# Output and down projection in four column groups, with rows of y as their result

## The chip, the cores and the metric

The kernel runs on one core of a Trainium2 chip. The metric is the device time of one execution in microseconds. Before the change it is 201.81 us, the median of three runs (201.67 to 201.96).

## The reference

A decode step for 8 sequences of one token, D = 512. The input x is layer-normalised, and two branches use the result: sliding-window attention with 32 query heads and 8 key/value heads over the last W = 2048 of 8192 cached positions, and a gated unit with F = 1792. The output joins them.

```python
xn = layernorm(x)                                     # x: [8, 1, 512]
q  = xn @ wq                                          # 32 heads of 128
k, v = the last 2048 rows of the caches, each shared by 4 query heads
o  = softmax(q k^T / sqrt(128)) v
s  = o.reshape(8, 1, 4096) @ wo                       # the output projection, [8, 512]
h  = sigmoid(xn @ w_gate) * (xn @ w_up)               # [8, 1792]
g  = silu(h @ w_down)                                 # the down projection, [8, 512]
return x + s * g
```

All is bfloat16 in memory. The windows of the two caches are 64 MB together and the weights some 14 MB.

## The kernel before, in words

**Loads.** A ring of 14 buffers of 128 x 4096 bf16 (1 MB) takes everything that is read but x: the halves of w_gate, w_up and w_down (896 KB each), four tiles of Wq, 32 tiles of K, 32 of V, and four of Wo. The list is written out by hand: the weights of the unit, Wq, then K tiles with the V tiles seven places behind, then Wo. The transfers are issued in turn from ACT's and from SP's queue (`load`, line 87), each as soon as the tile that had the buffer before is reported as used (`done_with`). The first three Wo tiles are one transfer each; the fourth is cut into two pieces of 512 KB, one for each queue (`wo_parts`, lines 114 to 119). Instructions on an engine are carried out in the order of the program, DMA issues among them. The built program lets all transfers share eight completion semaphores in turn, so that each issue also waits until the transfer eight places before it has landed.

**Start.** x is loaded to eight partitions and normalised; four TensorE transpositions give xnT (line 229), four more give xT, the columns of x (line 238), which DVE copies to SBUF (line 242). The unit (lines 245 to 291): 56 matmuls each for gate and up (line 253) give d_ps, DVE multiplies sigmoid and up to hT (line 270), and 56 matmuls of the down projection (line 278) give b_ps, in which a partition is a column of y: the weights are the stationary operand (128 x 128), hT streams through with 8 columns. Sigmoid and product (lines 288, 290) give gg. Then the q projection (line 297), and the copies of q into a zero-padded buffer qz (line 328), done in turn by ACT and DVE.

**Attention.** Each step n of one loop takes K tile n through DVE's transposition (line 343), the score matmuls of tile n - 1 (line 364: 8 of 512 columns), and the V products of tile n - 7 (line 434: 32 of 8 columns). Every four steps close one sequence: maximum (lines 376 to 389), exponentials on ACT (line 393), transposition of the probabilities (line 407), denominator (lines 415 to 426). A K buffer is free when it has been transposed, a V buffer when its products are done.

**End.** `out_rows` (line 451) brings the attention output from the order of the heads into rows of Wo, with 16 matmuls of an identity in four column groups (32 columns of weights each, placed by `tile_position`), and DVE copies that to o2 (line 461). `out_project` (line 472) runs 128 matmuls, each with a 128 x 128 block of Wo as the stationary operand and 8 columns of o2 streaming; the result a_ps has columns of y on its partitions. Then the product with gg (line 507), the addition of xT (line 509), a TensorE transposition (line 513), a copy (line 517), and one store of 32 rows of 256 bytes from SP's queue (line 518).

Of the kernel before, what the change touches and what calls it, by code (L numbers as in the profile page):

```python
# [10 lines left out]
def kernel(  # L11
# [13 lines left out]
    nc = tc.nc  # L25
    P = 128
    B, _, D = A_x.shape
# [6 lines left out]
    FT = F // P  # L34
    NB = D // P
    HG = Hq // 4
# [18 lines left out]
    bf16 = mybir.dt.bfloat16  # L55
    f32 = mybir.dt.float32
    u32 = mybir.dt.uint32
    AF = mybir.ActivationFunctionType
    ALU = mybir.AluOpType
# [6 lines left out]
    work = ctx.enter_context(tc.tile_pool(name="work", bufs=1))  # L66
# [3 lines left out]
    psum = ctx.enter_context(  # L70
        tc.tile_pool(name="psum", bufs=2, space=bass.MemoryType.PSUM)
    )
# [5 lines left out]
    x_bf = work.tile([B, D], bf16, name="x_bf")  # L78
    nc.sync.dma_start(out=x_bf[:], in_=A_x.flatten_outer_dims())

    queues = [nc.scalar, nc.sync]
# [32 lines left out]
    def wo_parts(h):  # L114
        v = A_wo.rearrange("(hg p j) n -> p hg (j n)", p=P, j=4)
        w = 4 * D
        g0 = h * HG // 4
        cuts = ((0, 2),) if h < 3 else ((0, 1), (1, 2))
        return [(lo * w, hi * w, v[:, g0 + lo : g0 + hi, :]) for lo, hi in cuts]

    loads = []
    for key, w, parts in (
# [9 lines left out]
    for _, kind, m in need:  # L132
        cache = A_v_cache if kind else A_k_cache
        loads.append((("v" if kind else "k", m), lambda cache=cache, m=m: kv_parts(cache, m)))
    loads += [(("wo", h), lambda h=h: wo_parts(h)) for h in range(4)]
    issued = [0]

# [8 lines left out]
    def done_with(*key):  # L146
        used[key] = True
        issue_loads()
# [4 lines left out]
    ident = consts.tile([P, P], bf16, name="ident")  # L153
# [3 lines left out]
    for off in range(-Hq * (NU - 1), Hq * NU, Hq):  # L157
        nc.gpsimd.affine_select(
            out=SumM[:],
            in_=SumM[:],  # L160
# [10 lines left out]
    for j in range(NU):  # L171
# [5 lines left out]
        out=off_rows[:],  # L177
        in_=off_rows[:],
# [9 lines left out]
        out=off_cols[:],  # L188
        in_=off_cols[:],
# [23 lines left out]
        out=rstd[:], in_=mv[:, 1:2], func=AF.Sqrt, bias=eps_t[:], scale=1.0  # L213
# [4 lines left out]
        out=xn_bf[:],  # L218
        in0=x_f[:],
# [8 lines left out]
    for kt in range(KT):  # L228
        nc.tensor.transpose(  # L229
            out=xnT_ps[:, kt, :], in_=xn_bf[:B, kt::KT], identity=ident[:B, :B]  # L230
# [2 lines left out]
    nc.vector.tensor_copy(out=xnT_sb[:], in_=xnT_ps[:])  # L233


    xT_ps = psum.tile([P, NB, B], bf16, name="xT_ps", tag="s1")
    for nb in range(NB):
        nc.tensor.transpose(
            out=xT_ps[:, nb, :], in_=x_bf[:B, nb * P : (nb + 1) * P], identity=ident[:B, :B]
        )  # L240
    xT_sb = work.tile([P, NB, B], f32, name="xT_sb")
    nc.vector.tensor_copy(out=xT_sb[:], in_=xT_ps[:])


    def unit_half(key, tag):
        w_sb = [
            tiles[(key, h)][:, : KT * F // 2].rearrange("p (kt f) -> p kt f", kt=KT // 2)
            for h in range(2)
        ]
        d_ps = psum.tile([P, FT, B], f32, name="d_ps", tag=tag)  # L250
        for t in range(FT):
            for kt in range(KT):
                nc.tensor.matmul(  # L253
                    d_ps[:, t, :],
                    lhsT=w_sb[2 * kt // KT][:, kt % (KT // 2), t::FT],
                    rhs=xnT_sb[:, kt, :],
                    start=(kt == 0),
                    stop=(kt == KT - 1),
                )
        done_with(key, 0)  # L260
        done_with(key, 1)
        return d_ps

    def unit():
        g_ps = unit_half("wg", "s0")
        sig = work.tile([P, FT, B], f32, name="sig")
        nc.scalar.activation(out=sig[:], in_=g_ps[:], func=AF.Sigmoid)
        u_ps = unit_half("wu", "s1")
        hT_sb = work.tile([P, FT, B], bf16, name="hT_sb")
        nc.vector.tensor_tensor(out=hT_sb[:], in0=sig[:], in1=u_ps[:], op=ALU.mult)  # L270
        wd_sb = [
            tiles[("wd", h)][:, : FT * D // 2].rearrange("p (t n) -> p t n", t=FT // 2)
            for h in range(2)
        ]
        b_ps = psum.tile([P, NB, B], f32, name="b_ps", tag="s0")
        for nb in range(NB):
            for t in range(FT):
                nc.tensor.matmul(
                    b_ps[:, nb, :],
                    lhsT=wd_sb[2 * t // FT][:, t % (FT // 2), nb * P : (nb + 1) * P],  # L280
                    rhs=hT_sb[:, t, :],
                    start=(t == 0),
                    stop=(t == FT - 1),
                )
        done_with("wd", 0)
        done_with("wd", 1)
        sigb = work.tile([P, NB, B], f32, name="sigb")
        nc.scalar.activation(out=sigb[:], in_=b_ps[:], func=AF.Sigmoid)
        gg_sb = work.tile([P, NB, B], f32, name="gg_sb")
        nc.vector.tensor_tensor(out=gg_sb[:], in0=sigb[:], in1=b_ps[:], op=ALU.mult)  # L290
        return gg_sb

# [151 lines left out]
        )  # L444


    def out_rows():
        o2_ps = psum1.tile([P, 4, B, HG], f32, name="o2_ps", tag="misc")
        for hl in range(4):
            for j in range(4):  # L450
                nc.tensor.matmul(
                    o2_ps[32 * hl : 32 * (hl + 1), j, :, :],
                    lhsT=ident[:, j::4],
                    rhs=oT_sb[:, :, hl::4],
                    start=True,
                    stop=True,
                    tile_position=(0, 32 * hl),
                    skip_group_check=True,
                )
        o2_sb = work.tile([P, HG, 4, B], bf16, name="o2_sb")  # L460
        nc.vector.tensor_copy(out=o2_sb[:].rearrange("p hg j b -> p j b hg"), in_=o2_ps[:])
        return o2_sb

    def out_project(o2_sb):

        a_ps = psum.tile([P, NB, B], f32, name="a_ps", tag="s0")
        for hg in range(HG):
            w_sb = tiles[("wo", 4 * hg // HG)]
            for j in range(4):
                for nb in range(NB):  # L470
                    c0 = ((hg % (HG // 4)) * 4 + j) * D + nb * P
                    nc.tensor.matmul(  # L472
                        a_ps[:, nb, :],
                        lhsT=w_sb[:, c0 : c0 + P],
                        rhs=o2_sb[:, hg, j, :],
                        start=(hg == 0 and j == 0 and nb == 0),
                        stop=(hg == HG - 1 and j == 3),
                        skip_group_check=True,
                    )
        return a_ps  # L480

    gg_sb = unit()
    q_projection()
    mj_of = {}
    dh_of = {}
    for n in range(NT + V_LAG):
        b, ph = divmod(n - NI, NI)
# [14 lines left out]
            soft_den(b, dh_of.pop(b))  # L502


    a_ps = out_project(out_rows())
    prod = work.tile([P, NB, B], f32, name="prod")
    nc.vector.tensor_tensor(out=prod[:], in0=gg_sb[:], in1=a_ps[:], op=ALU.mult)
    yT_sb = work.tile([P, B, NB], bf16, name="yT_sb")
    nc.vector.tensor_tensor(
        out=yT_sb[:].rearrange("p b nb -> p nb b"), in0=prod[:], in1=xT_sb[:], op=ALU.add  # L510
    )
    y_ps = psum.tile([B * NB, P], bf16, name="y_ps", tag="s1")
    nc.tensor.transpose(
        out=y_ps[:], in_=yT_sb[:].rearrange("p b nb -> p (b nb)"), identity=ident[:, :]
    )
    y_sb = work.tile([B * NB, P], bf16, name="y_sb")
    nc.vector.tensor_copy(out=y_sb[:], in_=y_ps[:])
    nc.sync.dma_start(
        out=out.rearrange("b s (nb n) -> (b s nb) n", n=P), in_=y_sb[:]
    )  # L520


# [28 lines left out]
```

## Time and profile before

| quantity | value |
|---|---|
| time, median of three runs | 201.81 us (201.67 to 201.96) |
| time of the profiled execution | 201.71 us |
| its span, first to last instruction | 200.0 us |
| read from memory | 81.01 MB, 405 GB/s over the span |
| busy: PE, DVE, ACT | 64%, 57%, 9% |
| mean granted TensorE clock | 0.874 |

The span is cut into 40 slices of 5 us in the page's rows by slices: the DMA row is the busy share of the core's 16 DMA engines in tenths, and the GB/s row what they moved. In the chain that ended last each row has a start in us, a length in us, and what took that time; "issue" is time without a cause that the profile shows. In the timeline a row has the start, the length, the engine, the line and operation, the result and operands with their shape (partitions x elements), the number of instructions, and in brackets the idle time before and what ended it. Rows of stretches (us from the span's start) give the busy time of PE, PEld, DVE, ACT and POOL with the number of instructions, then the granted clock, the DMA share and GB/s. PEld is the loading of weights, which overlaps PE. The time from a DMA's issue to its landing is also in the trace, for every transfer.

### The profile page before, as it was taken

To read this page: it belongs to the slowest core of one execution; us is meant where nothing else is said; L and a number is where in the kernel's file an instruction comes from. 1 tells how busy PE (TensorE), PEld (TensorE's weight loads), DVE (VectorE), ACT (ScalarE), POOL (GpSimd) and SP (SyncE) were. 2 spreads that over 40 slices of the span, in tenths; PEclk is the share of its full clock that TensorE was granted. 3 is DMA by queue.
4 is the path that set the end of the run, shared out by engine and by line. 5 is a ranking of instruction groups with operands and counts; after the bars stand their busy time and mean duration, and the time that the engine had idled before them with its cause. 6 is when DMAs were issued, how large, how long until landed. Compare 5 with 4: busy or idle time off the path is not lost.

```text
span 200.0 us, 4098 instructions
## 1 busy us (share of the span) xinstructions
PE 127.2 (64%) x1793; PEld 76.3 (38%) x1793; DVE 114.5 (57%) x199; ACT 18.7 (9%) x46; POOL 14.2 (7%) x25
## 2 busy tenths in 40 slices
PE   0004948004995796996796996369644965594943
PEld 0004946001332443644353553225322633254843
DVE  2001001049998787997977997386746784717221
ACT  0003300040022002002000200110002000202000
POOL 7991000000000000000000000000000000000000
PEclk9999999999999797899888899959995899588555
DMA  6999999999999999999999999999999999999970
GB/s 205 427 425 430 429 421 424 424 428 431 426 423 429 426 426 429 419 426 423 428 421 429 428 424 428 421 429 428 423 428 428 426 419 428 426 421 424 416 299 11
DMA packets 11842, 81.29 MB, mean 406 GB/s; under 512 B 1320, under 2 KB 1328, under 8 KB 3120
## 3 DMA queue, kind: packets, MB, share of 16 engines
q10 hardware_dynamic: 6016, 41.03, 49.1%
q1 hardware_dynamic: 5808, 40.00, 47.5%
q8 instruction: 14, 0.23, 0.4%
q14 instruction: 4, 0.03, 0.0%
HBM read 81.01 MB, written 0.01 MB: 405 GB/s over the span
## 4 chain that ended last, share of the span: by engine, by line
DMA 74%; PE 11%; DVE 9%; ACT 2%; issue 1%; ACTq 1%; DVEq 0%
DMA v_sb<-in_A_v_cache_dram 48%; DMA wo_sb<-in_A_wo_dram 10%; DMA k_sb<-in_A_k_cache_dram 9%; PE s_ps L364 7%; DMA wd_sb<-in_B_w_down_dram 6%; DVE kT_sb L343 5%; PE d_ps L253 2%; DVE qz_sb L328 1%; DVE mxs L376 1%; ACTq L87 1%; ACT qz_sb L328 1%; PE a_ps L472 1%; PE o_ps L434 1%; ACT L212 1%; DVE pT_sb L407 1%
## 5 line engine op out<-in xcount | busy, mean ns | idle before, releaser
L364 PE MATMUL s_ps<-kT_sb,qz_sb 128*128 128x512 bf16 x256 | 74.9, 439 | 12.6 <-DVE kT_sb L343 12.6
L343 DVE STREAM_TRANSPOSE kT_sb<-k_sb 128x1024 uint32<-128x1024 uint32 x64 | 74.6, 1210 | 0.0
L364 PEld LDWEIGHTS <-qz_sb 128*128 128x128 bf16 x256 | 25.4, 110 | 46.8 <-issue 30.9
L434 PEld LDWEIGHTS <-v_sb 128*128 128x128 bf16 x1024 | 30.8, 99 | 6.7 <-issue 2.9
L434 PE MATMUL o_ps<-pT_sb,v_sb 128*128 128x8 bf16 x1024 | 30.3, 167 | 0.0
L393 ACT ACTIVATE p_bf<-s_ps,nm 128x512 bf16<-128x512 f32 x16 | 10.9, 683 | 112.7 <-DVE nm L389 41.3
L424 PE MATMUL den_ps<-dh,ones 128*128 128x32 f32 x16 | 4.2, 349 | 20.5 <-DVE dh L417 20.4
L407 DVE STREAM_TRANSPOSE pT_sb<-p_bf 128x512 bf16<-128x512 bf16 x16 | 10.6, 690 | 10.4 <-ACT p_bf L393 10.3
L442 DVE TENSOR_TENSOR oT_sb<-o_ps,rden 128x8 bf16<-128x8 f32 x32 | 5.3, 166 | 17.4 <-PE o_ps L434 16.9
L229 PE MATMUL xnT_ps<-ident,xn_bf 8*128 8x8 bf16 x4 | 0.3, 175 | 17.6 <-DVE xn_bf L217 17.6
L424 PEld LDWEIGHTS den_ps<-dh,ones 128*128 128x128 f32 x16 | 3.2, 249 | 21.6 <-DVE dh L417 21.5
L387 PE MATMUL mb_ps<-mj,SumM 128*128 128x4 f32 x16 | 3.1, 263 | 12.4 <-DVE mj L380 12.4
L376 DVE TENSOR_REDUCE mxs<-s_ps 128x1 f32<-128x512 f32 x16 | 10.1, 668 | 0.0
L328 DVE CAST qz_sb<-qx_ps 32x256 bf16<-32x256 f32 x8 | 3.1, 418 | 9.9 <-ACT qz_sb L328 9.9
L387 PEld LDWEIGHTS mb_ps<-mj,SumM 128*128 128x128 f32 x16 | 2.4, 188 | 15.9 <-DVE mj L380 15.9
L215 DVE RECIPROCAL rstd<-rstd 8x1 f32<-8x1 f32 x1 | 0.2, 151 | 13.0 <-ACT rstd L212 13.0
L200 POOL MEMSET qz_sb<- 128x8320 f32 x1 | 7.0, 7021 | 0.0
L229 PEld LDWEIGHTS <-xn_bf 8*128 8x128 bf16 x4 | 0.2, 115 | 17.6 <-DVE xn_bf L217 17.6
L352 PE MATMUL s_ps<-off_cols,off_rows 2*128 2x512 bf16 x16 | 6.6, 412 | 0.0
L472 PE MATMUL a_ps<-o_sb,wo_sb 128*128 128x8 bf16 x128 | 3.7, 168 | 3.1 <-DMA wo_sb<-in_A_wo_dram 1.6
L426 DVE RECIPROCAL rden<-den_ps 128x32 f32<-128x32 f32 x8 | 2.9, 358 | 4.1 <-PE den_ps L424 4.1
L297 PE MATMUL qT_ps<-xnT_sb,wq_sb 128*128 128x8 bf16 x128 | 3.7, 168 | 2.1 <-DMA wq_sb<-in_A_wq_dram 2.1
(59 smaller groups left out, 59.3 us busy)
## 6 DMA issues: line engine op xcount, KB each, us to landing
k_sb<-in_A_k_cache_dram SPq DMA_DIRECT2D x28, 1024.0 KB, 19.5
v_sb<-in_A_v_cache_dram ACTq DMA_DIRECT2D x28, 1024.0 KB, 19.5
k_sb<-in_A_k_cache_dram ACTq DMA_DIRECT2D x4, 1024.0 KB, 20.0
v_sb<-in_A_v_cache_dram SPq DMA_DIRECT2D x4, 1024.0 KB, 19.5
wq_sb<-in_A_wq_dram ACTq DMA_DIRECT2D x2, 1024.0 KB, 17.2
wq_sb<-in_A_wq_dram SPq DMA_DIRECT2D x2, 1024.0 KB, 18.7
wo_sb<-in_A_wo_dram ACTq DMA_DIRECT2D x2, 1024.0 KB, 20.5
wo_sb<-in_A_wo_dram SPq DMA_DIRECT2D x1, 1024.0 KB, 18.7
```

Of the source, the lines that this page charges most:

```text
L200: nc.gpsimd.memset(qz_sb[:].rearrange("p b w -> p (b w)").bitcast(f32), 0.0)
L328: copy(out=dst[:, :, :, c0 : c0 + HT], in_=src)
L343: nc.vector.transpose(out=kT[:], in_=tiles[("k", m)][:, cols].bitcast(u32))
L352: nc.tensor.matmul(s_tiles[(b, u)][:], lhsT=off_rows[:].rearrange("k a j r -> k (a j r)"), rhs=off_cols[:].rearrange("k a j -> k (a j)"), ...
L364: nc.tensor.matmul(s_tiles[(b, u)][:], lhsT=qz_sb[:, b, c0 : c0 + P], rhs=kv[:, x // 2, x % 2], start=False, stop=(i == NI - 1 and x == NX ...
L376: nc.vector.reduce_max(out=mxs[:, u : u + 1], in_=s_tiles[(b, u)][:], axis=AX.X)
L387: nc.tensor.matmul(mb_ps[:], lhsT=SumM[:], rhs=mj[:], start=True, stop=True)
L393: nc.scalar.activation(out=p_bf[:, u, :], in_=s_tiles.pop((b, u))[:], func=AF.Exp, bias=nm[:], scale=scale, accum_out=dens[:, u : u + 1],)
L407: nc.vector.transpose(out=pT_tiles[b][:, u * CPS : (u + 1) * CPS, :].rearrange("p c h -> p (c h)"), in_=p_bf[:, u, :],)
L424: nc.tensor.matmul(den_ps[:], lhsT=ones[:], rhs=dh[:], start=True, stop=True)
L434: nc.tensor.matmul(o_ps[:], lhsT=tiles[("v", m)][:, c * Dh : (c + 1) * Dh], rhs=pT_tiles[b][:, c, hs], start=(c == 0), stop=(c == C - 1),)
L472: nc.tensor.matmul(a_ps[:, nb, :], lhsT=w_sb[:, c0 : c0 + P], rhs=o2_sb[:, hg, j, :], start=(hg == 0 and j == 0 and nb == 0), stop=(hg == ...
```

## The change

The two projections swap their operands: hT and o2 (now padded with zeros from 8 to 32 columns) become the stationary operand, and the weights stream through, 128 columns at a time. The 512 columns of y are cut in four blocks nb, and block nb goes to column group nb of the array (partitions 32 nb to 32 nb + 31 of the result, of which 8 are used), with the four blocks as the innermost loop. b_ps and a_ps so hold rows of y: sequence b and block nb stand on partition 32 nb + b, as 128 columns. gg, the product and the sum become 128 x 128 operations (they were 128 x 32).

x is wanted in the same layout: the four transpositions of x and their copy go, and instead four loads from SP's queue fetch x as blocks (8 rows of 256 bytes each) into a zeroed tile, which DVE casts to f32. These loads stand in the program behind the first loads of the ring, and the cast stands on DVE ahead of the unit. The last transposition and its copy go; the sum is written as bf16 and stored by four stores, two from ACT's queue and two from SP's.

The fourth Wo tile is loaded in three pieces: 512 KB, 256 KB and 256 KB, the last one before on ACT now being one half on each queue.

```diff
@@ wo_parts
-        cuts = ((0, 2),) if h < 3 else ((0, 1), (1, 2))
-        return [(lo * w, hi * w, v[:, g0 + lo : g0 + hi, :]) for lo, hi in cuts]
+        if h < 3:
+            return [(0, 2 * w, v[:, g0 : g0 + 2, :])]
+        return [(0, w, v[:, g0, :])] + [
+            (w + lo * w // 2, w + (lo + 1) * w // 2, v[:, g0 + 1, lo * w // 2 : (lo + 1) * w // 2])
+            for lo in range(2)
+        ]
@@ start
-    xT_ps = psum.tile([P, NB, B], bf16, name="xT_ps", tag="s1")
-    for nb in range(NB):
-        nc.tensor.transpose(
-            out=xT_ps[:, nb, :], in_=x_bf[:B, nb * P : (nb + 1) * P], identity=ident[:B, :B]
-        )
-    xT_sb = work.tile([P, NB, B], f32, name="xT_sb")
-    nc.vector.tensor_copy(out=xT_sb[:], in_=xT_ps[:])
+    def blocks(t, dram):
+        d = dram.rearrange("b s (nb n) -> nb (b s) n", n=P)
+        return [(t[32 * nb : 32 * nb + B, :], d[nb]) for nb in range(NB)]
+
+    x_blocks = work.tile([P, P], bf16, name="x_blocks")
+    nc.vector.memzero(x_blocks[:])
+    for dst, src in blocks(x_blocks, A_x):
+        nc.sync.dma_start(out=dst, in_=src)
+    xb_f = work.tile([P, P], f32, name="xb_f")
+    nc.vector.tensor_copy(out=xb_f[:], in_=x_blocks[:])
@@ unit
-        hT_sb = work.tile([P, FT, B], bf16, name="hT_sb")
-        nc.vector.tensor_tensor(out=hT_sb[:], in0=sig[:], in1=u_ps[:], op=ALU.mult)
+        hT_sb = work.tile([P, FT, 32], bf16, name="hT_sb")
+        nc.vector.memzero(hT_sb[:])
+        nc.vector.tensor_tensor(out=hT_sb[:, :, :B], in0=sig[:], in1=u_ps[:], op=ALU.mult)
...
-        for nb in range(NB):
-            for t in range(FT):
+        for t in range(FT):
+            for nb in range(NB):
                 nc.tensor.matmul(
-                    b_ps[:, nb, :],
-                    lhsT=wd_sb[2 * t // FT][:, t % (FT // 2), nb * P : (nb + 1) * P],
-                    rhs=hT_sb[:, t, :],
+                    b_ps[32 * nb : 32 * (nb + 1), :],
+                    lhsT=hT_sb[:, t, :],
+                    rhs=wd_sb[2 * t // FT][:, t % (FT // 2), nb * P : (nb + 1) * P],
                     start=(t == 0),
                     stop=(t == FT - 1),
+                    tile_position=(0, 32 * nb),
...
@@ end
+    o2_sb = work.tile([P, HG, 4, 32], bf16, name="o2_sb")
+    nc.vector.memzero(o2_sb[:])
...
+        nc.vector.tensor_copy(
+            out=o2_sb[:, :, :, :B].rearrange("p hg j b -> p j b hg"), in_=o2_ps[:]
+        )
...
-                        a_ps[:, nb, :],
-                        lhsT=w_sb[:, c0 : c0 + P],
-                        rhs=o2_sb[:, hg, j, :],
-                        start=(hg == 0 and j == 0 and nb == 0),
+                        a_ps[32 * nb : 32 * (nb + 1), :],
+                        lhsT=o2_sb[:, hg, j, :],
+                        rhs=w_sb[:, c0 : c0 + P],
+                        start=(hg == 0 and j == 0),
                         stop=(hg == HG - 1 and j == 3),
+                        tile_position=(0, 32 * nb),
...
-    nc.tensor.transpose(
-        out=y_ps[:], in_=yT_sb[:].rearrange("p b nb -> p (b nb)"), identity=ident[:, :]
-    )
-    y_sb = work.tile([B * NB, P], bf16, name="y_sb")
-    nc.vector.tensor_copy(out=y_sb[:], in_=y_ps[:])
-    nc.sync.dma_start(
-        out=out.rearrange("b s (nb n) -> (b s nb) n", n=P), in_=y_sb[:]
-    )
+    y_bf = work.tile([P, P], bf16, name="y_bf")
+    nc.vector.tensor_tensor(out=y_bf[:], in0=prod[:], in1=xb_f[:], op=ALU.add)
+    for n, (src, dst) in enumerate(blocks(y_bf, out)):
+        queues[n % 2].dma_start(out=dst, in_=src)
```

## The prediction

> **What bounds the kernel now.** The page first: its rows of the DMA engines by slices of 5 us, and the shares of the chain that ended last.
>
> ```profile
> DMA  6999999999999999999999999999999999999970
> GB/s 205 427 425 430 429 421 424 424 428 431 426 423 429 426 426 429 419 426 423 428 421 429 428 424 428 421 429 428 423 428 428 426 419 428 426 421 424 416 299 11
> DMA 74%; PE 11%; DVE 9%; ACT 2%; issue 1%; ACTq 1%; DVEq 0%
> ```
>
> The transfers run at about 425 GB/s from 2 us to 190 us without a gap. So all that the compute engines do before the weights end costs nothing unless a queue runs dry. Next the chain from 174 us, in order of time:
>
> ```profile
> 174.17 20.50 DMA wo_sb<-in_A_wo_dram
> 194.66 0.05 issue
> 194.71 1.88 PE a_ps L472 x64
> 196.59 0.02 issue
> 196.61 0.20 DVE prod L507
> 196.81 0.02 issue
> 196.83 0.24 DVE yT_sb L509
> 197.07 0.04 issue
> 197.12 0.30 PE y_ps L513
> 197.41 0.02 issue
> 197.44 0.21 DVE y_sb L517
> ```
>
> The third Wo tile (ACT queue) lands at 194.67; PE then does 64 matmuls without a stop, which is half of the projection. The two 512 KB pieces land at 177.94 + 16.55 = 194.5 and 179.02 + 16.84 = 195.9, and PE comes to the last piece at about 194.71 + 48 x 0.027 = 196.0, so that piece is not waited for (0.1 us to spare). After PE there is 1.1 us of four short steps, the store (issued at 197.68, 1.4 us to landing) and 0.9 us to the span's end. Last the timeline, for the rows that carry prices:
>
> ```profile
> 25.14 0.27 DVE L270 TENSOR_TENSOR hT_sb<-sig,d_ps 128x112 bf16<-128x112 f32 x1 [6.87 <-PE d_ps L253]
> 25.47 1.63 PE L278 MATMUL b_ps<-hT_sb,wd_sb 128*128 128x8 bf16 x56 [0.44 <-DVE hT_sb L270]
> 41.00 0.63 ACT L328 CAST qz_sb<-qx_ps 32x256 bf16<-32x256 f32 x2 [9.72 <-DMA k_sb<-in_A_k_cache_dram]
> 46.20 2.37 DVE L343 STREAM_TRANSPOSE kT_sb<-k_sb 128x1024 uint32<-128x1024 uint32 x2
> 172.77 3.60 PE L364 MATMUL s_ps<-kT_sb,qz_sb 128*128 128x512 bf16 x8
> 189.32 0.46 PE L451 MATMUL o_ps<-oT_sb,ident 128*32 128x64 bf16 x16 [0.26 <-DVE oT_sb L442]
> ```
>
> The reader should see in them that hT was ready at 25 us, that the qz copies waited for a DMA issue on ACT's queue until 41 us (9.72), and that the K transposes start at 46.2.
>
> **The end, step by step** (against the profiled execution: 201.71 us, span 200.0; the median of three is 0.1 higher).
>
> Matmuls of the last 64. Before: (1.87 - 0.17) / 63 = 27 ns each. After, each streams 128 columns instead of 8, in one of four column groups. The granted clock is 0.50 from 183.6 us to the end. At 0.50 the scores row above gives 3.60 / 8 = 0.45 us for 512 columns, so 0.112 us for 128. The out_rows row is the same form (32 columns of weights, four groups) at the same clock: (0.46 - 0.24) / 15 = 15 ns each for 64 columns, where one after the other would be 56 ns; so four run side by side, weight loads included. Four matmuls of 128 columns then take 0.112, 28 ns each: 63 x 1 ns = +0.05. The last matmul's own duration is 0.17 for 8 columns, 0.24 for 64, so about 0.29 for 128: +0.1, less the 0.08 by which its group of four starts together. Taken: +0.05 in all. Bounds: -0.85 at full clock (a scores row of 8 at clock 1.00 takes 1.89 us, half), +5.4 if the groups run one after the other (64 x 0.112 = 7.2 for 1.8). I take the out_rows row, being nearest in form, clock and place.
>
> The Trainium skill speaks against this step: by TensorEngine Tiling (Array Packing), "Gotcha 2: Feature Incompatibilities", column tiling excludes Fast Weight Load, and TensorE: Matmul & The Clock Gate, "LDWEIGHTS (loading the stationary operand)", prices a plain load at columns / 1.2 ns, 27 ns for 32. Its Part 3, "The mechanism", has loads overlap running matmuls only where the row group differs, which column groups do not have. By those rules four loads of 107 ns would stand beside each four matmuls, an estimate of +1.7 us and a time of 203.5; no run here shows it, and the 15 ns of out_rows speak against it.
>
> prod (L507): 0.19 for 32 elements, and the sig product reads PSUM the same way at 0.27 for 112; so 0.29 for 128: +0.10. The addition: 0.23 now (32 elements, strided write), 0.29 by the same line, contiguous: +0.05. Gone are the gap, transposition, gap and copy between 197.07 and the issue at 197.68: -0.62. Four stores, two on each queue: issues on SP at the start stand at 0.80, 1.25, 1.66, 2.12, so the second store of a queue goes 0.43 later: +0.43 (bounds: 0, if the second is hidden; 0.54, the issue of a full tile). Sum: +0.05 + 0.10 + 0.05 - 0.62 + 0.43 = 0.0 us.
>
> The Wo pieces. The half tile that was one 512 KB transfer on ACT is 256 KB on each queue. SP now has something left when its 512 KB piece lands at 194.5, so it shares with ACT's third tile for 0.17 us: +0.1 on the landing that PE waits for. The last bytes are the same, so the smaller last piece gains only where PE waits for it, which it does not. ACT's half is one place later in the turn of the semaphores: it waits for the V tile issued on SP at 163.2 (19.5 to landing, 182.7) and not 179.0, and ACT's last exponentials, now at 182.31, stand behind it: 0.8 late. The final V products and the first 64 matmuls follow 0.8 late and end at 193.9; PE waited 1.58 us for Wo, so 0.8 of cover is left. Cost 0; without cover it would be 0.8.
>
> **The start.** Four transposes and a copy (0.4 us) go; the added instructions are four x-block loads, three memsets and a cast. The cast stands on DVE ahead of hT and waits for all four loads; they are on SP's queue behind the K tile issued at 18.17 (20.9 to landing: 39.1). The last of them must itself wait for the first K tile (issued at 10.40, 20.0: 30.4), and SP's K tiles behind them go later too: 23.1 becomes 34.1, 29.3 becomes 39.1. SP still holds a megabyte each time, and a tile takes 4.9 us per queue. ACT's V tile waits for the first x block instead of a K tile, also 39.1, and for the down projection.
> From 39.2: cast 0.2 (like L233's 0.17), two memsets 0.5 (between eps's 0.06 and POOL's 0.52 each), hT 0.27, down projection 1.63 + 0.1, q projection 3.50 (L297), qT 0.42, qx 1.05: 46.9. The qz copies then, at 41.0 before: 5.9 us late, and the K transposes at 52.1.
> What covers that: a tile issued into a full queue takes 19.5 to 19.8 us to landing; the tightest ones were the K tile at 69.58 (13.6) and the V tile at 64.56 (14.9). A queue is dry when only its own 4.9 us are left, at 13.6 - 4.9 = 8.7 us of delay. 5.9 leaves 2.8. The delay is made good: a batch takes DVE about 15 us (L376 at 59.87, 75.25, 90.13), and 8.4 MB at 425 GB/s 19.7 us. So 0, bounds 0 (the loads land at once: 0.5 us late) and +2 (10.7 us late). I take 0.
> The loads themselves are 32 packets of 256 B. By bytes they cost nothing; as average packets (200 x 16 / 11842 = 0.27 us each, over 16 engines) 0.5 us. Taken: 0.1. The o2 copy (1.27, L461) writes with a longer stride, under PE's 1.58 us of waiting.
>
> Sum: 0.0 + 0.1 + 0.1 = +0.2 on 201.71: **201.9 us**.
>
> **Rivals.**
> *Ring starved (slower).* The start is later than 8.7 us, and the loads pause around 70 to 80 us. For it: the margin is 2.8 us, and PE starts the scores cold. Against: each queue alone can fill the engines. At 10 to 12 us late: +1.3 to +3.3, 203.2 to 205.
> *Weights exposed or groups serial (slower).* Against it: the out_rows row. From +1 (15 ns more per matmul) to +5.4: 203 to 207.
> *A ragged end that moves (both ways).* The engines empty one after the other:
>
> ```profile
> 192.00:192.50 0.50, 0.50 (x25) 0.50 (x22) 0.00 (x0) 0.00 (x0) 0.00 (x0) 0.50 0.96 377
> 192.50:193.00 0.50, 0.50 (x24) 0.50 (x21) 0.00 (x0) 0.00 (x0) 0.00 (x0) 0.50 0.65 262
> 194.00:194.25 0.25, 0.00 (x0) 0.00 (x0) 0.00 (x0) 0.00 (x0) 0.00 (x0) 0.50 0.29 115
> 195.50:196.00 0.50, 0.50 (x25) 0.50 (x22) 0.00 (x0) 0.00 (x0) 0.00 (x0) 0.50 0.16 33
> ```
>
> Last but one is the DMA share. By the landing records of the last Wo transfer, seven engines were done by 193.4, four by 194.4, five by 195.9: steps of 1.2 us, as a few packets of instructions (14 on their own queue) might make. If the changed program or its other order of transfers takes one step from the slowest five, both the third tile and the last bytes come 1.2 earlier: about 200.8. If it adds one: 203.1.
>
> **Chances.** The sum as told 0.52 (its own range 201.4 to 202.4; same 0.42, slower 0.08, faster 0.02); ring starved 0.13; weights or groups 0.07; ragged end shorter 0.20, longer 0.08. Faster 0.22, within 0.2% (0.4 us, about what this kernel's runs, 201.67 to 201.96, can tell from no change) 0.42, slower 0.36. The range 200.8 to 203.2 leaves out half of the starved case, most of the serial one and the far parts of the ragged ones.
>
> **What would show it.** Right: the DMA row without a gap, hT at about 40 us, K transposes at about 52, the last 64 matmuls 1.8 to 2.0 us long, 0.6 us gone between the addition and the first store's issue, the last store landing 0.4 later than the first. Wrong: a slice of 5 us between 60 and 90 us below 415 GB/s; matmuls of L472's successor over 35 ns apart; hT before 35 us (then the loads did not queue); a third Wo tile that lands before 193.5 or after 195.5.

## The result, and the profile after

| | changed kernel | kernel before |
|---|---|---|
| median | 202.79 us (202.56 to 203.41, 7 runs) | 202.03 us (201.67 to 202.17, 7 runs on the same chip) |
| ratio, 95% interval | 1.0046 (1.0031 to 1.0060) | |
| profiled execution | 203.27 us, span 201.5 us | 201.71 us, span 200.0 us |

The change makes the kernel 0.46% slower, about 0.8 us. The forecast was 201.9 us with the range 200.8 to 203.2: the time lies inside the range, but on the side of a rival, not at the likeliest value. The profiled execution is one of the slower ones of the seven, so it shows the loss at the upper end of its size.

First the rate of the transfers by slices of 5 us, from the page of the changed kernel:

```profile
GB/s 205 424 429 425 429 423 428 425 428 420 433 425 425 425 428 376 348 425 423 423 428 426 426 426 423 428 425 428 428 423 426 421 426 426 431 423 417 417 317 11
```

Before, no slice between 5 and 190 us was below 416. Now the slices from 75 to 85 us have 376 and 348 in place of some 426: (50 + 78) x 5 / 426 = 1.5 us of transfer time lost. Stretches of 1 us around it (the last two columns are the DMA share and GB/s):

```profile
77.00:78.00 1.00, 1.00 (x6) 0.48 (x5) 1.00 (x1) 0.00 (x0) 0.00 (x0) 1.00 0.91 295
78.00:79.00 1.00, 1.00 (x31) 0.77 (x28) 1.00 (x2) 0.00 (x0) 0.00 (x0) 1.00 1.09 459
...
80.00:81.00 1.00, 1.00 (x5) 0.27 (x4) 1.00 (x2) 0.00 (x0) 0.00 (x0) 1.00 0.74 246
81.00:82.00 1.00, 0.85 (x4) 0.19 (x2) 1.00 (x2) 0.00 (x0) 0.00 (x0) 1.00 0.95 344
82.00:83.00 1.00, 0.00 (x0) 0.00 (x0) 0.96 (x3) 0.00 (x0) 0.00 (x0) 1.00 0.97 303
83.00:84.00 1.00, 0.57 (x16) 0.57 (x17) 0.49 (x3) 0.00 (x0) 0.00 (x0) 1.00 0.83 320
```

That is the pause "around 70 to 80 us" of the rival *Ring starved*. The start that leads to it, from the timeline:

```profile
39.19 0.23 DVE L249 CAST xb_f<-x_blocks 128x128 f32<-128x128 bf16 x1 [20.67 <-DMA x_blocks<-in_A_x_dram]
40.33 0.27 DVE L278 TENSOR_TENSOR hT_sb<-sig,d_ps 128x112 bf16<-128x112 f32 x1
40.66 1.68 PE L286 MATMUL b_ps<-wd_sb,hT_sb 128*32 128x128 bf16 x56 [15.33 <-DVE hT_sb L278]
47.38 0.63 ACT L338 CAST qz_sb<-qx_ps 32x256 bf16<-32x256 f32 x2 [4.71 <-PE qx_ps L322]
52.57 4.62 DVE L353 STREAM_TRANSPOSE kT_sb<-k_sb 128x1024 uint32<-128x1024 uint32 x4
```

DVE stands for 20.67 us at the cast, hT comes 15 us later than before, and the K transpositions begin at 52.57 where they began at 46.20: 6.4 us late. The end, from the timeline:

```profile
181.62 0.16 DVE L399 TENSOR_REDUCE nm<-mb_ps 128x1 f32<-128x4 f32 x1 [0.48 <-PE mb_ps L397]
...
185.03 0.35 ACTq L87 DMA_DIRECT2D wo_sb<-in_A_wo_dram  x1
185.48 0.69 ACT L403 ACTIVATE p_bf<-s_ps,nm 128x512 bf16<-128x512 f32 x1 [14.36 <-DMA v_sb<-in_A_v_cache_dram]
...
192.33 0.46 PE L464 MATMUL o_ps<-oT_sb,ident 128*32 128x64 bf16 x16 [0.26 <-DVE oT_sb L452]
192.87 1.29 DVE L473 CAST o_sb<-o_ps 128x256 bf16<-128x256 f32 x1 [0.60 <-PE o_ps L464]
194.22 3.85 PE L484 MATMUL a_ps<-wo_sb,o_sb 128*32 128x128 bf16 x128 [1.43 <-DVE o_sb L473]
198.11 0.29 DVE L521 TENSOR_TENSOR prod<-gg_sb,a_ps 128x128 f32<-128x128 f32 x1 [3.95 <-PE a_ps L484]
198.44 0.29 DVE L523 TENSOR_TENSOR y_bf<-prod,xb_f 128x128 bf16<-128x128 f32 x1
198.75 0.68 SPq L525 DMA_DIRECT2D out_dram<-y_bf  x2
198.76 0.99 ACTq L525 DMA_DIRECT2D out_dram<-y_bf  x2
```

Two things are late here at once. The negated maximum nm, which the last exponentials need, is ready at 181.78, but they begin at 185.48: ACT first has to issue its 256 KB of Wo (185.03), and that issue waits for a V tile on SP that lands at 184.96. And the weights are late: by the landing records the last pieces of Wo are there at 197.41 and 197.57, where before the last one was there at 195.87. From the end of PE's work to the end of the span it takes 3.4 us in both kernels (196.59 to 200.0 before, 198.09 to 201.5 now), so what was done to the steps behind the projection cancels out.

So there were two suspects: the late start (a dry ring at 75 to 85 us), and the new cut of the last Wo tile (held exponentials). The runs take them apart. In each one the median is set against runs of the kernel before on the same chip (201.69 to 201.78 us).

### The profile page after: what moved, and what is told of

It reads as the page before. It is cut to its first block, busy times and chain, and to the rows that moved or that the text cites. A ratio compares the mean times of both kernels' runs of the same rounds, so it can differ in the third digit from the quotient of the medians.

```text
span 201.5 us, 4101 instructions
## 1 busy us (share of the span) xinstructions
PE 127.3 (63%) x1788; PEld 76.0 (38%) x1788; DVE 115.1 (57%) x201; ACT 18.8 (9%) x46; POOL 14.3 (7%) x25
## 4 chain that ended last, share of the span: by engine, by line
DMA 63%; DVE 19%; PE 13%; issue 2%; ACT 1%; ACTq 0%; DVEq 0%; SPq 0%
DMA k_sb<-in_A_k_cache_dram 39%; DVE kT_sb L353 11%; DMA v_sb<-in_A_v_cache_dram 9%; DMA wo_sb<-in_A_wo_dram 6%; PE s_ps L374 6%; DMA wu_sb<-in_B_w_up_dram 5%; DMA x_blocks<-in_A_x_dram 4%; PE o_ps L444 3%; DVE mxs L386 2%; DVE pT_sb L417 2%; PE qT_ps L307 2%; DVE qz_sb L338 1%; PE b_ps L286 1%; ACT qz_sb L338 1%; PE den_ps L434 1%
## 5 line engine op out<-in xcount | busy, mean ns | idle before, releaser
L249 DVE CAST xb_f<-x_blocks 128x128 f32<-128x128 bf16 x1 | 0.2, 228 | 20.7 <-DMA x_blocks<-in_A_x_dram 20.7
L286 PE MATMUL b_ps<-wd_sb,hT_sb 128*32 128x128 bf16 x56 | 1.7, 312 | 15.3 <-DVE hT_sb L278 15.3
L286 PEld LDWEIGHTS <-hT_sb 128*32 128x32 bf16 x56 | 1.4, 144 | 15.4 <-DVE hT_sb L278 15.4
```

The lines of the kernel that those rows point to most:

```text
L286: nc.tensor.matmul(b_ps[32 * nb : 32 * (nb + 1), :], lhsT=hT_sb[:, t, :], rhs=wd_sb[2 * t // FT][:, t % (FT // 2), nb * P : (nb + 1) * P], ...
```

## Experiments on the start

**The cast moved out of the way.** Only the place of the cast in DVE's order changes; the x loads stay where they are.

```diff
     for dst, src in blocks(x_blocks, A_x):
         nc.sync.dma_start(out=dst, in_=src)
-    xb_f = work.tile([P, P], f32, name="xb_f")
-    nc.vector.tensor_copy(out=xb_f[:], in_=x_blocks[:])
...  (ahead of out_rows(), behind the attention loop)
+    xb_f = work.tile([P, P], f32, name="xb_f")
+    nc.vector.tensor_copy(out=xb_f[:], in_=x_blocks[:])
```

> The changed kernel with only the cast of the x blocks moved: it stands behind the attention loop and no longer ahead of hT. The loads of the x blocks stay where they are, behind the K tile on SP's queue. Theory A (the cast holds DVE until 39 us, all compute starts 6.4 us late, and the transfers run dry between 75 and 85 us): hT at about 26 us, K transposes at 46 to 48, no slice of 5 us below 415 GB/s between 60 and 90 us, time within 0.3 us of before (about 202.0). Theory B (the small loads disturb the order of the transfers on SP's queue, whatever DVE does): the dip stays, 202.6 to 203. Theory C (the loss is at the end: stores, wider DVE steps, column groups): no dip or not, the time stays at 202.6 to 203.

Measured: 201.82 us (201.49 to 201.89, 11 runs), ratio 1.0000 (0.9992 to 1.0009). The whole loss is gone. hT stands at 26.65, the K transpositions begin at 47.13, and no slice dips. From its page the rates by slices, and from its timeline the K transpositions and the end:

```profile
GB/s 195 420 428 429 427 421 429 424 422 432 427 419 432 427 421 427 426 426 426 424 424 426 429 424 427 426 424 429 426 421 432 429 418 426 431 418 423 413 305 14
...
47.13 13.63 DVE L351 STREAM_TRANSPOSE kT_sb<-k_sb 128x1024 uint32<-128x1024 uint32 x12
...
184.03 0.69 ACT L401 ACTIVATE p_bf<-s_ps,nm 128x512 bf16<-128x512 f32 x1 [12.52 <-DMA v_sb<-in_A_v_cache_dram]
...
192.77 1.90 PE L482 MATMUL a_ps<-wo_sb,o_sb 128*32 128x128 bf16 x64 [1.44 <-DVE o_sb L471]
194.83 1.93 PE L482 MATMUL a_ps<-wo_sb,o_sb 128*32 128x128 bf16 x64 [0.17 <-DMA wo_sb<-in_A_wo_dram]
```

The exponentials are still held, now by 1.2 us (nm is ready at 182.85), and 0.17 us of PE's waiting for Wo are left of the 1.58 us of before: the cover is just used up.

**The x loads first.** The zeroing and the four x loads go ahead of the first load of the ring, so they land early; the cast stays where the change put it.

```diff
...  (blocks() moves up as well; the same lines go at their old place)
+    x_blocks = work.tile([P, P], bf16, name="x_blocks")
+    nc.vector.memzero(x_blocks[:])
+    for dst, src in blocks(x_blocks, A_x):
+        nc.sync.dma_start(out=dst, in_=src)
     queues = [nc.scalar, nc.sync]
```

> The changed kernel with the zeroing and the four loads of the x blocks moved ahead of all loads of the ring; the cast stays ahead of hT. Theory A: the cast ends before 20 us, hT at about 26 us, no dip, time about 202.0; SP's first ring load goes some 1.5 us later, which costs nothing as long as ACT's queue keeps the engines busy. Theory B also gives about 202.0 here, since nothing small stands between the K tiles. Theory C: 202.6 to 203.

Measured: 202.87 us (202.73 to 203.01, 5 runs), ratio 1.0055 (1.0042 to 1.0067). A miss for the theory of one cause: hT is ready at 23.61, the K transpositions begin at 43.95, earlier than in the kernel before, no slice dips, and still the loss is there in full. From the timeline of its end:

```profile
178.90 0.16 DVE L399 TENSOR_REDUCE nm<-mb_ps 128x1 f32<-128x4 f32 x1 [0.68 <-PE mb_ps L397]
...
184.34 0.35 ACTq L95 DMA_DIRECT2D wo_sb<-in_A_wo_dram  x1
184.79 0.69 ACT L403 ACTIVATE p_bf<-s_ps,nm 128x512 bf16<-128x512 f32 x1 [15.98 <-DMA v_sb<-in_A_v_cache_dram]
...
193.52 3.78 PE L484 MATMUL a_ps<-wo_sb,o_sb 128*32 128x128 bf16 x128 [1.43 <-DVE o_sb L473]
```

The exponentials could start at 179.06 and start at 184.79: 5.7 us held behind ACT's issue. PE then goes through all 128 matmuls without a stop, although the last of Wo is there at 196.10 and the third tile at 193.43; it is the attention's end that is late, not the weights. This made the second suspect a cause, which the run with the old cut and the x loads first confirms (below).

**The late start alone.** The kernel before, with the zeroing, the four loads and the cast of the changed kernel at their place; nothing reads the result, so the output is that of the kernel before.

```diff
...  (blocks() as in the changed kernel)
+    x_blocks = work.tile([P, P], bf16, name="x_blocks")
+    nc.vector.memzero(x_blocks[:])
+    for dst, src in blocks(x_blocks, A_x):
+        nc.sync.dma_start(out=dst, in_=src)
+    xb_f = work.tile([P, P], f32, name="xb_f")
+    nc.vector.tensor_copy(out=xb_f[:], in_=x_blocks[:])
```

> The kernel before with the start of the change alone: zeroing, the four loads of x blocks and the cast, at the same place in the program; their result is not used, and the transpositions of x and the end stay as before. Theory A: K transposes at about 52 us, a dip between 70 and 85 us, 0.7 to 1.5 us slower than before (202.7 to 203.5). Theory B gives the same. Theory C: no slower than before by more than 0.2.

Measured: 201.80 us (201.53 to 202.84, 11 runs), ratio 1.0011 (0.9997 to 1.0024). The cast waits as long as in the changed kernel, hT is there at 39.34, but without the two zero-fills ahead of hT (0.72 us) the K transpositions begin at 51.45, 5.25 us late, and the profiled execution has no dip. Two of the eleven executions took 202.8. The expected loss of 0.7 to 1.5 us did not come: 5.25 us of lateness is mostly free, and perhaps near an edge.

**DVE late, and nothing else.** The kernel before with memsets of a scratch tile on DVE ahead of hT, 22 of them in one run and 19 in another; their result is not used.

```diff
+        idle = work.tile([P, 1024], f32, name="idle")
+        for _ in range(22):
+            nc.vector.memset(idle[:], 0.0)
```

> The kernel before with 22 zeroings of a scratch tile (128 x 1024 f32, about 1 us each) on DVE ahead of hT, and no other change: no small loads, the same order of transfers, hT at about 40 us as in the changed kernel. Theory A: K transposes at about 52 us, a dip between 70 and 85 us, 0.7 to 1.5 us slower than before. Theory B: no dip, the time of before within 0.3 us. Theory C: the time of before.

> The kernel before with 19 memsets on DVE ahead of hT, of which nothing uses the result (22 of them gave 207.25, K transposes 10 late): K transposes at about 52.7, some 6.5 us later than in the kernel before, which is the lateness of the changed kernel (6.4) with none of its other edits. By the prediction's margin (8.7 us of delay before the queues are dry): 201.7 to 202.0, no dip. By a margin of about 5 us at the K transposes (the first landing on the fast engines, and about 1.2 us from an issue to its first bytes, taken off): a dip between 70 and 85 us and 202.5 to 204.

Measured: with 22, which took 1.19 us each and so delayed more than was meant, K transpositions at 56.19, 207.25 us (206.74 to 207.71, 4 runs), ratio 1.0272 (1.0256 to 1.0288). With 19, K transpositions at 53.08, 203.25 us (202.97 to 204.67, 6 runs), ratio 1.0091 (1.0067 to 1.0115). The rates by slices, of the run with 22 memsets:

```profile
GB/s 223 422 426 432 427 420 428 427 329 313 412 432 427 417 427 312 358 395 422 425 427 424 425 428 425 425 425 432 420 428 420 427 425 425 425 427 424 410 330 12
```

and of the run with 19:

```profile
GB/s 203 428 423 430 431 419 432 423 426 410 432 423 429 418 431 350 389 429 421 427 423 431 419 434 418 432 421 429 426 424 424 423 426 429 421 429 420 412 245 8
```

The dip at 75 to 85 us comes back at the same place with nothing but lateness on DVE. With 22 memsets there is a second one at 40 to 50 us: after a K tile issued at 29.02 the next transfer is issued at 45.88, as the down projection, begun at 44.39, comes to its end, and the last one under way lands at 46.59. The profiled executions together, with the run of the old cut that is told below (the loss is the execution's own time less the median of the kernel before beside it; the time lost in dips is reckoned from the slices as above):

| run | K transpositions begin | late by | loss | lost in dips | late by, less the loss |
|---|---|---|---|---|---|
| late start alone | 51.45 | 5.2 | 0.0 | 0.0 | |
| changed kernel | 52.57 | 6.4 | 1.2 | 1.5 | 5.1 |
| 19 memsets | 53.08 | 6.9 | 2.5 | 1.3 | 4.4 |
| changed kernel, old cut | 53.38 | 7.2 | 2.4 | 1.4 | 4.8 |
| 22 memsets | 56.19 | 10.0 | 5.0 | 5.3, half of it at 40 to 50 us | 5.0 |

In these five executions some 5 us of lateness are free, and the rest comes back as time. That it does so nearly one for one is rough: the executions of one kernel lie up to 1.9 us apart, and in the third and fourth row the dips make up only about half of the loss. The other half, about 1 us, came at the end, where the last piece of Wo lands in sixteen parts over 4.0 and 4.1 us (3.4 before, 3.1 in the changed kernel); no run shows why. The prediction had 8.7 us free.

## Experiments on the cut of Wo

**The old cut in the changed kernel.**

```diff
-        if h < 3:
-            return [(0, 2 * w, v[:, g0 : g0 + 2, :])]
-        return [(0, w, v[:, g0, :])] + [...]
+        cuts = ((0, 2),) if h < 3 else ((0, 1), (1, 2))
+        return [(lo * w, hi * w, v[:, g0 + lo : g0 + hi, :]) for lo, hi in cuts]
```

> The changed kernel with the old cut of the last Wo tile (two pieces of 512 KB), everything else as changed. Two-cause theory (a late start that runs the ring dry by up to 1.5 us, and a last Wo cut that holds ACT's last exponentials behind a V tile's landing): ACT issues its piece at about 179 us without a V tile on SP ahead of it, the exponentials go as soon as nm is there (about 182 instead of 185.48), but the late start stays (xb_f cast near 39.2, K transposes near 52.5) and with it a dip at 75 to 85 us in some executions; 201.8 to 202.5, below the changed kernel's 202.79 by 0.3 to 1.0. If the starved ring alone made the loss: 202.6 to 203.0, exponentials early and nothing gained. If the cut alone made it: 201.6 to 201.9.

Measured: 203.44 us (202.41 to 204.35, 6 runs), ratio 1.0077 (1.0049 to 1.0105). The time lies above everything that was expected. The exponentials are free, and nothing is gained:

```profile
GB/s 220 422 431 428 424 427 424 429 421 429 423 432 419 431 424 337 393 423 426 423 426 426 424 431 419 431 419 432 421 429 424 427 421 431 421 428 415 416 231 7
...
182.36 0.69 ACT L399 ACTIVATE p_bf<-s_ps,nm 128x512 bf16<-128x512 f32 x1 [10.66 <-DVE nm L395]
...
194.81 1.05 PE L480 MATMUL a_ps<-wo_sb,o_sb 128*32 128x128 bf16 x32 [2.09 <-DMA wo_sb<-in_A_wo_dram]
196.95 1.99 PE L480 MATMUL a_ps<-wo_sb,o_sb 128*32 128x128 bf16 x64 [1.09 <-DMA wo_sb<-in_A_wo_dram]
```

PE waits 2.09 and 1.09 us for Wo, whose last piece lands at 198.28. In the changed kernel itself, too, the chain that ended last goes through Wo:

```profile
185.03 12.37 DMA wo_sb<-in_A_wo_dram
197.41 0.04 issue
197.45 0.64 PE a_ps L484 x16
```

So in the changed kernel as it is, the late weights are what ends last; the held exponentials lie beside them. PE ends 0.52 us behind the last landing there (197.57 to 198.09), and 0.44 behind it in a run below whose exponentials are free, so freeing them would gain some 0.1 us at most. The run with the old cut had a start that was later still (ACT's copies of qz at 48.19 instead of 47.38, behind two DMA issues that took 2.24 us instead of 1.49), but its dip is no deeper. What it loses beyond the changed kernel lies in the ragged end told above; whether the cut has a part in that was not tried.

**The old cut with the x loads first.** The edit above made to the run with the x loads first.

> The changed kernel with the x loads ahead of the ring's loads, and the old cut of the last Wo tile: the run with the x loads first (202.87, ratio 1.0055) with one further edit. If the cut is what that run lost by: exponentials at about 179 to 180 instead of 184.79, PE waits for Wo again and not for the exponentials, 201.4 to 201.9. If that run lost by having four small loads at the head of SP's queue (the turn of the queues, other semaphores, a ragged end): 202.6 to 203.0, whatever the exponentials do.

Measured: 201.93 us (201.76 to 202.51, 8 runs), ratio 1.0016 (1.0006 to 1.0026), against 1.0055 with the new cut. The profiled execution is the slowest of the eight (202.51). In it the exponentials begin at 180.22 on nm, and PE waits for Wo twice (0.67 and 0.54 us). With an early start, the cut alone makes the 0.9 us.

**The new cut in the kernel before.**

```diff
-        cuts = ((0, 2),) if h < 3 else ((0, 1), (1, 2))
-        return [(lo * w, hi * w, v[:, g0 + lo : g0 + hi, :]) for lo, hi in cuts]
+        if h < 3:
+            return [(0, 2 * w, v[:, g0 : g0 + 2, :])]
+        return [(0, w, v[:, g0, :])] + [...]
```

> The kernel before with the last Wo tile cut into 512, 256 and 256 KB and nothing else. ACT's 256 KB issue then waits for the V tile issued on SP at 163.2, landing 182.7, and the exponentials begin at about 183.2 instead of 182.31, 0.9 late. If 1.58 us of waiting for Wo covers that, as the prediction has it: 201.7 to 202.1, with the gap before the last 64 matmuls shrunk to about 0.6. If the cut is worth more than its lateness here: 202.4 to 203. A gain, 201.2 to 201.6, if the smaller last piece is worth something by itself.

Measured: 201.83 us (201.66 to 202.05, 11 runs), ratio 1.0005 (0.9996 to 1.0013).

```profile
183.35 0.69 ACT L397 ACTIVATE p_bf<-s_ps,nm 128x512 bf16<-128x512 f32 x1 [12.03 <-DMA v_sb<-in_A_v_cache_dram]
...
192.16 1.85 PE L476 MATMUL a_ps<-o_sb,wo_sb 128*128 128x8 bf16 x64 [1.51 <-DVE o_sb L465]
194.74 1.80 PEld L476 LDWEIGHTS <-wo_sb 128*128 128x128 bf16 x64 [0.82 <-DMA wo_sb<-in_A_wo_dram]
```

Here the prediction's step holds: 183.35 where 182.31 + 0.8 was worked out, and 0.8 us of PE's waiting for Wo left. The same cut costs nothing here, some 0.1 us at most in the changed kernel, and 0.9 us with the x loads first, depending on when nm is ready (182.0 here, 181.78 and 179.06 there) and when Wo lands.

**The three pieces on SP.** With the x loads first, and in the kernel before with the new cut added, all pieces of the last Wo tile are issued from SP, so that ACT issues nothing behind its third tile.

```diff
         for lo, hi, src in parts:
-            load(t[:, lo:hi], src)
+            if key == ("wo", 3):
+                nc.sync.dma_start(out=t[:, lo:hi], in_=src)
+            else:
+                load(t[:, lo:hi], src)
```

> The changed kernel with the x loads ahead of the ring's loads and all three pieces of the last Wo tile issued from SP, so that ACT issues nothing after the third Wo tile. If the exponentials held behind ACT's issue are the loss: exponentials at about 179 to 180, PE waits for Wo only, and the small last piece may now gain: PE ends at 196.0 to 196.5, 201.2 to 201.8. If the small pieces or the loads at the head of SP's queue are the loss: 202.6 to 203.0. If one queue alone moves the last megabyte slower: Wo's last landing later than 196.5 and 202 to 202.6 with early exponentials.

> The kernel before with the last Wo tile cut into 512, 256 and 256 KB and all three issued from SP, nothing else. The kernel with this cut on SP and the changed layout with its x loads first took 201.38. If that gain comes from the pieces on SP (both queues' last landings closer together, the exponentials free): 201.3 to 201.6. If it comes from the new layout or the earlier start: 201.7 to 201.9. If one queue moves the last megabyte slower: over 202.

Measured: with the x loads first 201.38 us (201.18 to 201.90, 11 runs), ratio 0.9985 (0.9977 to 0.9994); in the kernel before 201.88 us (201.69 to 202.04, 11 runs), ratio 1.0007 (0.9998 to 1.0016). The first is the only version faster than the kernel before, by 0.15%: the interval leaves out 1, though the size is under the 0.2% named above as telling. From its timeline:

```profile
180.11 0.69 ACT L406 ACTIVATE p_bf<-s_ps,nm 128x512 bf16<-128x512 f32 x1 [11.46 <-DVE nm L402]
...
191.46 1.04 PE L487 MATMUL a_ps<-wo_sb,o_sb 128*32 128x128 bf16 x32 [1.43 <-DVE o_sb L476]
193.18 3.08 PE L487 MATMUL a_ps<-wo_sb,o_sb 128*32 128x128 bf16 x96 [0.67 <-DMA wo_sb<-in_A_wo_dram]
```

With the same three pieces on both queues it was 202.87, so what costs 1.5 us there is the issue on ACT and not the size of the pieces. The third Wo tile is there at 193.24, the last 256 KB at 195.82, and PE ends at 196.26, 0.44 later. With the old cut and the x loads first it ended 1.08 behind the last 512 KB (196.26 to 197.34). So the smaller last piece is worth about 0.6 us where that piece is what ends last. In the kernel before it is not: PE has to wait for the third tile there until 194.73 and then has 64 matmuls to do, whatever the last piece's size.

## Experiments with a larger ring

The changed kernel with 15 buffers instead of 14, once as it is and once with the old cut.

```diff
-    RING = 14
+    RING = 15
```

> The changed kernel as it is, with a fifteenth buffer in the ring: the new cut and the late start both stay, only the dry ring should go. If the dry ring is all of the loss: 201.8 to 202.1, the same as with the old cut and 15 buffers, the exponentials still behind ACT's issue (about 183.5 to 184) and PE still waiting a few tenths for Wo. If the held exponentials cost beside it: 202.2 to 202.8, 0.4 or more above the old cut with 15 buffers, and PE goes through its 128 matmuls without a stop. If the ring is not it: 202.6 to 203.

> The changed kernel with the old cut of the last Wo tile (203.44) and a fifteenth buffer in the ring, so that every issue from the ring stands one tile earlier, with the start as late as before. If the late start loses its time by running the ring dry: the dip at 75 to 85 us goes or falls under 0.5 us and 201.8 to 202.2, 1.2 to 1.6 us less than with 14 buffers. If the late start costs in another way (the order on DVE or PE, the x loads): 203 to 203.6 as with 14.

Measured: 205.82 us (205.12 to 206.38, 4 runs), ratio 1.0200 (1.0181 to 1.0219), and with the old cut 206.14 us (205.08 to 207.02, 6 runs), ratio 1.0214 (1.0191 to 1.0237). None of the expectations had that. One half of the theory did come true. The rates of the run with the new cut:

```profile
GB/s 214 422 423 427 432 430 416 432 426 422 432 419 429 430 421 429 424 421 432 422 424 429 424 427 427 426 426 424 426 424 427 427 422 427 426 420 417 368 39 5
```

The dip is gone, and the last piece of Wo lands at 195.98, against 197.57 with 14 buffers and 195.87 in the kernel before. But now the attention is late:

```profile
149.77 5.41 ACTq L87 DMA_DIRECT2D v_sb<-in_A_v_cache_dram  x2
150.23 0.16 DVE L399 TENSOR_REDUCE nm<-mb_ps 128x1 f32<-128x4 f32 x1 [0.48 <-PE mb_ps L397]
155.28 0.69 ACT L403 ACTIVATE p_bf<-s_ps,nm 128x512 bf16<-128x512 f32 x1 [18.12 <-DMA k_sb<-in_A_k_cache_dram]
...
170.07 0.16 DVE L399 TENSOR_REDUCE nm<-mb_ps 128x1 f32<-128x4 f32 x1 [0.61 <-PE mb_ps L397]
175.34 0.69 ACT L403 ACTIVATE p_bf<-s_ps,nm 128x512 bf16<-128x512 f32 x1 [18.62 <-DMA v_sb<-in_A_v_cache_dram]
```

With a fuller ring ACT's issues of V tiles meet the wait for the transfer eight places before, inside the attention loop: the second of the two issues in the first row goes at 154.63, when the V tile issued eight transfers earlier, at 135.06, has landed (154.57). The exponentials of batches 5, 6 and 7 are held by 2.9, 4.9 and 5.1 us (by 0.1, 1.5 and 4.5 in the changed kernel with 14 buffers), the last nm comes at 188.1 instead of 181.8, and PE's projection starts at 197.13, behind all weights. The kernel before has holds of that kind too (5.8, 6.2 and 5.0 us in the same batches), but its batches start 6 us earlier, so its last nm is there at 182.2. The experiment so shows both ends of the same balance: what keeps the ring from running dry makes ACT wait longer. No run gave the kernel before a fifteenth buffer.

## Why the prediction was right or wrong

*The end, step by step*: right. The sum was 0.0, and from PE's end to the span's end it is 3.41 us before and after. Gone are the transposition and its gaps; SP's and ACT's stores land at 199.97 to 200.63. ACT's first store issue takes 0.65 us where SP's takes 0.32, so the last landing is 0.66 behind the first and not 0.4. prod and the addition take 0.29 each, as worked out.

*Matmuls of the last 64*: right. 1.90 and 1.93 us per 64 in the run with the late cast, 30 ns each, against 1.88 before; +0.05 was said. The rules of the Trainium skill that were weighed against it would have made +1.7 us (TensorEngine Tiling (Array Packing), "Gotcha 2: Feature Incompatibilities"; TensorE: Matmul & The Clock Gate, Part 3, "The mechanism"); the traces disagree, at 56 matmuls with 56 weight loads in 1.68 us and 128 in 3.34 to 3.85. That their 203.5 is not far from the result is chance.

*The Wo pieces*: the mechanism was right, and the size was not. "0.8 late" was said; the exponentials were held by 3.7 us in the changed kernel, 1.2 with the late cast, 1.4 with the cut alone, 5.7 with the x loads first. The step took both ends of that difference from the trace of before, the landing of one V tile and the 182.31 of the exponentials; but nm moves by some microseconds with the start, and the landing does not move with it. Its "cost 0" still holds, to some 0.1 us, for the changed kernel, but not for the reason given: the cover was not PE's 1.58 us but weights that came 1.7 us later.

*The start*: this is the step that failed. hT at 40.3, the qz copies at 47.4 and the K transpositions at 52.6 came as worked out to half a microsecond (40, 46.9, 52.1). "A queue is dry when only its own 4.9 us are left, at 13.6 - 4.9 = 8.7 us of delay. 5.9 leaves 2.8" was wrong: delay beyond about 5 us is paid. The 13.6 us were counted from an issue to the landing of its last part, on the slowest of the engines. In the trace of before, the K tile ahead of the one issued at 69.58 begins to land at 76.44 and ends at 78.23, so the first engines run out 6.9 us after that issue; and a transfer needs a start of its own: a store of 2 KB lands 1.2 us after its issue, and in the run with 22 memsets the issue at 45.88 that ends the first dip has its first packet at 47.20, 1.3 us later. 6.9 - 1.3 = 5.6 us, an estimate after the fact, which is near to what the runs show. On the way to that issue the delay also grew, from 6.4 us at the K transpositions to 7.2 (76.76 instead of 69.58). "Cost 0" should have been about +1, and the sum 203 instead of 201.9. The forecast held within its range because the range took in a part of the rivals; the step that decides the size of the loss was wrong. The loads of x themselves cost nothing that can be told: the late start alone has 1.0011.

*Ring starved*, the rival, had the place and the effect right (a pause at 70 to 80 us) and was given 0.13. The loss came by its mechanism, at a smaller size. Its condition, 10 to 12 us of delay for +1.3 to +3.3, went by the same wrong margin: 10 us cost 5.0 to 5.5.

*Weights or groups serial* did not happen. *A ragged end that moves* was not needed: with the cast late, the third Wo tile lands at 194.79 and the last piece at 196.22, within 0.4 of before. The ends that are about 1 us longer (19 memsets, old cut) are of its kind, but none of them is the changed kernel's.

Settled by the runs: the changed kernel's loss is the late start, since moving one cast takes it away whole, and lateness on DVE alone brings it about in the other kernel. The cut is a second cause that stands in wait behind it, and shows as soon as the first is mended in the way that makes nm early. Open is why the third Wo tile lands earlier with the x loads first: at 193.24 to 193.61 in the three runs that have them, with either cut and on either queue, against 194.66 before. The cut is not it (194.70 with the cut alone), and the changed layout by itself is not it either (194.79 with the cast late). ACT's third tile is issued at 171.58 to 172.05 in these runs and not at 174.17; whether the earlier start or the four loads at the head of SP's queue bring that was not taken apart.

## What to carry to other kernels

A small operand that is loaded behind a stream of megabyte tiles arrives behind the tile ahead of it (the first of the four x loads 18.5 us after its issue, where DVE stood for 20.7): load it first, or put the instruction that waits for it behind everything that the stream depends on. Reckon the slack of a prefetch ring from the first engine that runs out, and take off the time from an issue to its first bytes. And where a compute engine issues DMAs, ask for each issue what it waits for and which computation stands behind it; the cost hangs on when that computation becomes ready, so it must be worked out anew after every other edit.

## What the hardware showed that was not expected

The pace of the column-group matmuls does not follow the granted clock. At a granted clock of 1.00 the 56 matmuls of the down projection take 1.68 us, and at 0.50 the 128 of the output projection 3.85 us. A single one lasts 0.31, so they start (1.68 - 0.31) / 55 = 25 ns and (3.85 - 0.31) / 127 = 28 ns apart; the run with the old cut and 15 buffers has the 128 in 3.34 us at 0.50, less than in the changed kernel. The scores matmuls of the kernel before take 0.24 us at 1.00 and 0.45 at 0.50. From the stretches of the changed kernel (the first number behind the five engines is the granted clock):

```profile
40.00:42.00 2.00, 1.34 (x52) 1.35 (x56) 0.47 (x2) 0.00 (x0) 0.00 (x0) 1.00 1.02 430
194.00:196.00 2.00, 1.78 (x68) 1.78 (x72) 0.17 (x1) 0.00 (x0) 0.00 (x0) 0.50 0.62 232
```

The weight loads (PEld) are about as busy as the matmuls in both, 25 ns for each, which suggests that they and not the streaming set the pace; no run varied them.

A larger ring made the changed kernel 3 us slower (205.82 against 202.79) while it brought the last weights in 1.6 us earlier, because the transfers' completion semaphores, and not the buffers, became what an issue on ACT waits for.
